# Attention and a two-level mixture of experts on one core: query blocks transposed by VectorE, two PSUM copies on ScalarE, and a reordered end

## The chip, the core and the metric

The kernel runs on one core of a Trainium2 chip. A core has five engines with an instruction stream each: TensorE (PE, matrix products; its weight loads are listed as PEld), VectorE (DVE), ScalarE (ACT), GpSimd (POOL) and SyncE (SP, which here only issues DMAs). They wait for each other by semaphores. SBUF and PSUM are on-chip memories of 128 partitions; matmul results go to PSUM banks, which another engine has to copy out. The metric is the device time of one execution in microseconds (us). The time before is 558.53 us, the median of 3 runs (556.01 to 560.62).

## The reference, cut to what matters

First multi-query attention: 8 batches, 16 query heads, 384 tokens, head size 64, one key head and one value head that all query heads share. Then each of the 3072 tokens (1024 features, the 16 heads side by side) goes to one of 16 experts, chosen in two steps (4 groups, then 4 experts in the group).

```python
scores = scale * np.matmul(q, k.transpose(0, 1, 3, 2))
scores = scores - np.max(scores, axis=-1, keepdims=True)
attn = np.exp(scores)
attn = attn / (np.sum(attn, axis=-1, keepdims=True) + 1e-09)
attn_out = np.matmul(attn, v)
x = attn_out.transpose(0, 2, 1, 3).reshape(B * S, H * D)

g_logits = x @ w_group;  g_idx = argmax;  g_w = softmax(g_logits)[g_idx]
e_logits = x @ w_expert[g_idx];  e_idx = argmax;  e_w = softmax(e_logits)[e_idx]
out = g_w * e_w * (np.maximum(x @ w1[g, e], 0.0) @ w2[g, e])
```

All inputs are float32. With the inputs of this case nearly all tokens of a batch choose the same expert: one expert serves each of the first seven batches, and two serve the last.

## The kernel before, in words

**Tiles and slots.** The 384 tokens of a batch are three tiles of 128, so there are 24 tiles `t`. A tile has eight units (two heads each). The main loop runs over 96 slots `i`; a slot takes two units, so a tile is four slots, p = 0 to 3, and a batch is twelve.

**One slot.** TensorE forms the scores of the two units (L161). VectorE takes the row maxima (L169), ScalarE the exponentials with their sums (L172), VectorE the reciprocals (L183), GpSimd normalises (L187). Two slots later VectorE transposes the normalised rows in 32x32 blocks into a ring buffer (L193); that ring feeds the product with the values. Scores live in two PSUM buffers of two banks, one for each unit of a slot, which TensorE may write again when the exponentials have read them.

**What TensorE does besides.** In slots p = 0 and 1 it advances the expert of the batch before by two or three groups (`advance`; a group is 8 matmuls into one PSUM bank: L419 for the first weights, L433 for the second) and transposes queries (`q_group`, L147). In slots p = 2 and 3 it forms the product of the previous tile with the values (`pv`, L209, 96 matmuls in each of the two slots). All of these but the scores, and later the logits, take their banks in turn from four PSUM banks (`xbank`).

**Queries.** `load_q` brings a tile's queries with tokens on partitions: one DMA of 128 partitions by 16 heads by 64 numbers, into one of three buffers. `q_group` takes eight heads, transposes them pair by pair on TensorE against an identity into PSUM (four transposes), and ScalarE copies the result to SBUF (L151). The half needed later in tile `t` is made in slot 4t, the first half of tile t+1 in slot 4t+1. Tile `j` of a batch holds tokens p*3 + j for p = 0 to 127.

**Keys and values.** `prep_batch` transposes the keys of the next batch on TensorE in a batch's ninth slot; `prep_out` scales them by VectorE on the way out of PSUM (L135). `load_v` brings four copies of the values.

**After a tile's values.** `pv_out` copies four banks with ScalarE (L222), GpSimd casts to bf16 for the experts (L223). `logits` multiplies by the gate weights (L230), `logits_out` copies the result out of PSUM by VectorE (L239), `logits2` sums four partial rows on TensorE (L247), `logits2_out` copies that (L251). The gate functions (L256 to L388) run on VectorE at set slots, and the expert of a batch is picked after its first tile.

**Weights.** `load_w` asks GpSimd's DMA queue for an expert's two matrices (L394), two DMAs of 1 MB each, into two buffers per matrix. For batch b this is done behind slots 12b + 10 (the last batch: the second matrix one slot later). The last batch has a second expert: `load_second(0)` and `load_second(1)`.

**What sets the order.** The order on each engine is written out by hand: `at(slot, where, fn)` files a call under a slot and a letter, `run(slot, where)` makes the calls, and the loop at L603 fixes where the letters stand in a slot: scores, s, b, m0, m1 or values, v, m2, the ring transposes, w, `norm`, g. After the loop (L632 to L662) stands a hand-written end: remaining groups of the expert of batch 6, the last values, the last tile's logits and gate, the experts of batch 7, the second one's results added and stored in six pieces. A loop for further experts follows (L708); it has nothing to do with these inputs.

Of the kernel before, what the change touches and what calls it, by code (L numbers as in the profile page):

```python
# [9 lines left out]
FP32 = mybir.dt.float32  # L10
BF16 = mybir.dt.bfloat16
I32 = mybir.dt.int32
P = 128
AX = mybir.AxisListType
ALU = mybir.AluOpType
# [4 lines left out]
def kernel(  # L20
# [11 lines left out]
    nc = tc.nc  # L32
# [15 lines left out]


    xb_dram = nc.dram_tensor("xb_scratch", [B, P, KO * S], BF16).ap()  # L50
    out_v = out.rearrange("(b p j) d -> b p j d", p=P, j=ST)
    w1f = moe_w1.rearrange("g e (ko ki) f -> (g e) ki ko f", ki=P)
    w2f = moe_w2.rearrange("g e (fo fi) d -> (g e) fi fo d", fi=P)

# [29 lines left out]
    ring = singles.tile([P, 3, 4, 2, S], FP32)  # L84
    NB = S // 32

    def xbank():
        x = ps_x.tile([P, 512], FP32, tag="x", name="x")
        return x
# [5 lines left out]

    def load_q(t, first=False):
        b, j = t // ST, t % ST
        q_sb = qpool.tile([P, H, D], FP32, tag="q", bufs=3)
        qv = q[b].rearrange("h (p j) d -> p j h d", j=ST)
        if first:  # L100
            nc.sync.dma_start(out=q_sb[:, 0:H // 4, :], in_=qv[:, j, 0:H // 4, :])
            nc.scalar.dma_start(out=q_sb[:, H // 4:H // 2, :], in_=qv[:, j, H // 4:H // 2, :])
            nc.sync.dma_start(out=q_sb[:, H // 2:H, :], in_=qv[:, j, H // 2:H, :])
        else:
            nc.sync.dma_start(out=q_sb[:], in_=qv[:, j, :, :])
        st["q", t] = q_sb

    def load_k(b, first=False):
# [23 lines left out]
    def prep_out(b):  # L132
        pt = st.pop(("kt_ps", b))
        kt = qpool.tile([P, S], FP32, tag="kt")
        nc.vector.tensor_scalar(out=kt[:], in0=pt[:, 0:S], scalar1=scale, scalar2=None, op0=ALU.mult)  # L135
        st["kt", b] = kt

    def q_group(t, half, parts=1):
        q_sb = st["q", t]
        half ^= swapped(t)  # L140
        qt = pool.tile([P, 512], FP32, tag="qt", bufs=3)
        n = 4 // parts
        for part in range(parts):
            pt = xbank()
            for c in range(part * n, (part + 1) * n):
                h = 2 * (half * 4 + c)
                nc.tensor.transpose(  # L147
                    out=pt[:, ts(c, P)], in_=q_sb[:, h:h + 2, :].rearrange("p t d -> p (t d)"), identity=ident[:]
                )
            r = slice(part * n * P, (part + 1) * n * P)  # L150
            nc.scalar.copy(out=qt[:, r], in_=pt[:, r])  # L151
        st["qt", t, half] = qt

    def scores(u):
# [81 lines left out]

    def logits_out(b, j):
        lt = pool.tile([P, P], FP32, tag="lt")
        nc.vector.tensor_copy(out=lt[:], in_=st.pop(("lt_ps", b, j))[:, 0:P])  # L239
        if j == 0:  # L240
            st["lg", b] = pool.tile([P, ST, NL], FP32, tag="lg", name="lg")
        st["lt", b, j] = lt
# [228 lines left out]
    def main_expert(b, on_act):  # L471
        w1, w2 = st.pop(("w", b))

        def store(j, y):
            if b < B - 1:
                nc.sync.dma_start(out=out_v[b, :, j, :], in_=y[:])
            else:
                st["y", j] = y

        yield from expert(st["xb", b], w1, w2, scaled(lambda: st["gsel", b][0], store), any_bank, on_act)  # L480

    def second_expert(on_act):

        b = B - 1

        def result(j, nh, yp, by_act):
            y = st["y", j]
            nc.vector.scalar_tensor_tensor(
                out=y[:, ts(nh, 512)], in0=yp, scalar=st["gsel", b][1][:, j:j + 1], in1=y[:, ts(nh, 512)],
                op0=ALU.mult, op1=ALU.add,  # L490
            )
            nc.sync.dma_start(out=out_v[b, :, j, ts(nh, 512)], in_=y[:, ts(nh, 512)])

        yield from expert(st["xb", b], *st.pop("w_second"), result, any_bank, on_act)

# [20 lines left out]
    def at(slot, where, fn, *args):  # L516
        later.setdefault((slot, where), []).append((fn, args))
# [8 lines left out]
    for b in range(B):  # L526
        s0 = SB * b
        for j in range(ST):
            x = s0 + 4 * j + 8
            at(x, "m2", logits, b, j)  # L530
            at(x, "w", logits_out, b, j)
            at(x + 1, "m0", logits2, b, j)
            at(x + 1, "v", logits2_out, b, j)
        for x, j0, j1 in ((s0 + 9, 0, 1), (s0 + 17, 1, ST)):
            at(x, "v", lambda b=b, j0=j0, j1=j1: st.__setitem__(("gm", b), gate_masks(b, j0, j1)))
            at(x, "v", lambda b=b: [next(st["gm", b]) for _ in range(3)])
        if b == 0:
            at(s0 + 10, "s", gate_choose, b)
            at(s0 + 10, "b", gate_score, b)
        else:  # L540
            at(s0 + 9, "m2", gate_choose, b)
            at(s0 + 9, "w", gate_score, b)
        at(s0 + 10, "w", gate_pick, b)
        at(s0 + 10, "g", load_main, b, 0)
        at(s0 + (11 if b == B - 1 else 10), "g", load_main, b, 1)
        at(s0 + 16, "g", keep_xb, b)
        at(s0 + 20, "m0", gate_count, b)
        at(s0 + 20, "v", gate_counted, b)
        x = s0 + (20 if b == B - 2 else 23)
        at(x, "w", lambda b=b: st.__setitem__(("gv", b), gate_values(b)))  # L550
        at(x, "w", lambda b=b: [next(st["gv", b]) for _ in range(3)])
        if b == B - 1:
            at(s0 + 13, "w", gate_pick_second, b)
            at(s0 + 13, "g", load_second, 0)
        if b + 1 < B:
            at(s0 + 4, "g", load_k, b + 1)
            at(s0 + 4, "g", load_v, b + 1)
            at(s0 + 8, "m0", prep_batch, b + 1)
            at(s0 + 8, "v", prep_out, b + 1)
    for t in range(NT):  # L560
        at(4 * t, "m1", q_group, t, 1)
        if t + 1 < NT:
            at(4 * t + 1, "m1", q_group, t + 1, 0)
        if 1 <= t < NT - 2:
            at(4 * t, "g", load_q, t + 2)

    load_k(0, first=True)
# [31 lines left out]
    busy(1)  # L599
    q_group(0, 0, 2)  # L600
    load_v(0)
    load_q(2)
    for i in range(NSL):  # L603
        t, p = i // 4, i % 4
        if i >= SB + 5 and (i - 5) % SB == 0:
            pending.append(main_expert((i - 5) // SB - 1, lambda k: True))
        us = (2 * i, 2 * i + 1)
        for u in us:
            scores(u)
        run(i, "s")  # L610
        soft(us, lambda: run(i, "b"))
        if p < 2:
            run(i, "m0")
            advance(1)
            run(i, "m1")
            advance(2 if p == 1 and t % ST > 0 else 1)
        elif t > 0:
            pv(t - 1, (p - 2) * NB // 2, (p - 1) * NB // 2)
        run(i, "v")
        run(i, "m2")  # L620
        if i >= 2:
            transp(2 * i - 4)
            transp(2 * i - 3)
        run(i, "w")
        norm(us)
        if p == 3 and t > 0:
            pv_out(t - 1)
        run(i, "g")
# [10 lines left out]
    run(i, "w")  # L639
    transp(2 * i - 2)  # L640
    transp(2 * i - 1)
    advance(1)
    run(i + 1, "m0")
    run(i + 1, "v")
    run(i + 1, "w")
    run(i + 1, "g")
    pv(NT - 1, 0, NB)
    pv_out(NT - 1)
    advance(2)
    run(i + 4, "m2")  # L650
    run(i + 4, "w")
    run(i + 4, "g")
    advance(1)
    run(i + 5, "m0")
    run(i + 5, "v")
    pending.append(main_expert(b, lambda k: k < FO or k % 2 == 0))
    advance(1)
    load_second(1)
    pending.append(second_expert(None))
    advance(2)  # L660
    run(i + 8, "m0")
    run(i + 8, "v")  # L662

# [44 lines left out]
    with tc.For_i(0, n_rem, 1) as it:  # L708
        free.clear()
        e = nc.gpsimd.value_load(lse[0:1, ds(it, 1)], min_val=0, max_val=GE - 1)  # L710
        w1, w2 = load_w(e, 0), load_w(e, 1)
        bi = nc.sync.value_load(lsb[0:1, ds(it, 1)], min_val=0, max_val=B - 1)
        xr = pool.tile([P, KO, S], BF16, tag="xb", name="xr", bufs=2)
        nc.sync.dma_start(
            out=xr[:].rearrange("p c t -> p (c t)"), in_=xb_dram[ds(bi, 1)].rearrange("o p c -> (o p) c")
        )
        pid = nc.vector.value_load(lsi[0:1, ds(it, 1)], min_val=0, max_val=NP - 1)
        gcol = pool.tile([P, ST], FP32, tag="gcol")
        nc.vector.tensor_copy(out=gcol[:], in_=grem_all[:, ds(pid, 1), :].rearrange("p o j -> p (o j)"))
        bp = nc.gpsimd.value_load(lsb[0:1, ds(it, 1)], min_val=0, max_val=B - 1)  # L720

        def add(j, y):
            nc.gpsimd.dma_start(
                out=out_v[ds(bp, 1), :, j, :].rearrange("o p d -> (o p) d"), in_=y[:], accum_op=ALU.add
            )

        for _ in expert(xr, w1, w2, scaled(lambda: gcol, add), bank_end):
            pass
# [30 lines left out]
```

## Time and profile before

| what | value |
|---|---|
| median of 3 runs | 558.53 us |
| the profiled execution, its own time | 560.02 us |
| its span, first to last instruction | 558.58 us |
| TensorE (PE) busy | 530.6 us, 95% |
| VectorE (DVE) busy | 418.4 us, 75% |
| ScalarE (ACT) busy | 339.2 us, 61% |
| GpSimd (POOL) busy | 270.6 us, 48% |
| mean granted TensorE clock | 0.991 |
| moved by DMA | 75.15 MB |
| median from issue to landing: a tile's queries, 512 KB | 6.4 us |
| median from issue to landing: 1 MB of weights | 18.7 us |

The page lists for each group of instructions its source line, engine, operation, output and input tiles, their shapes, the count, then busy time and mean duration, then the engine's idle time just before them and what ended it. The chain is followed back from the last instruction: at each step to what released it, or else to the instruction before it on its engine; "issue" is time in which an engine waited for nothing that the profile shows. Matmuls are pipelined: on the chain a piece counts from its start to the start of the next. The windows view lists busy time of each engine in a stretch, then the granted clock, the share of the DMA engines and what they moved.

### The profile page before, as it was taken

The page shows a single profiled execution, that of the slowest core. Times are in us where ns is not written, and L with a number is a line of the kernel's source. Part 1 is how long each engine was busy: PE and PEld are TensorE (multiplying, and loading weights), DVE is VectorE, ACT ScalarE, POOL GpSimd, SP SyncE. Part 2 cuts the span into 40 slices and gives each one's busy share as a digit, 9 for nine tenths or more (in the row PEclk, how much of TensorE's full clock was granted, in tenths as well). Part 3 has the DMA queues.
Part 4 walks back from the last instruction along what each step waited for, and adds up shares of the span by engine and source line. Part 5 has one row for each costly group of instructions (what it writes and reads, how often), then busy time and mean ns, then how long its engine had stood idle before and what let it go on. Part 6 is the DMA issues. An engine that isn't in the chain of part 4 may idle for free.

```text
span 558.6 us, 17530 instructions
## 1 busy us (share of the span) xinstructions
PE 530.6 (95%) x7074; PEld 310.1 (56%) x7074; DVE 418.4 (75%) x847; ACT 339.2 (61%) x1043; POOL 270.6 (48%) x456
## 2 busy tenths in 40 slices
PE   7598899999999999999999999999999999979994
PEld 3255456655665556655665556655665555555452
DVE  4989988877888778877888678876888778823322
ACT  4776666666666666766666676676666676613210
POOL 2655954564457444565447535555447535622000
PEclk9999999999999999999999999999999999989999
DMA  7710993099805993099706992199706960299923
GB/s 118 161 30 13 177 229 75 2 195 233 202 2 97 210 250 77 4 200 247 181 1 111 213 262 48 11 211 247 164 2 111 213 189 2 29 212 263 222 51 115
DMA packets 98098, 75.15 MB, mean 135 GB/s; under 512 B 75104, under 2 KB 75104, under 8 KB 98016
## 3 DMA queue, kind: packets, MB, share of 16 engines
q0 software_dynamic: 19008, 37.75, 38.1%
q1 hardware_dynamic: 78080, 36.04, 24.7%
q8 instruction: 57, 0.93, 0.7%
q10 hardware_dynamic: 928, 0.23, 0.2%
q14 instruction: 25, 0.20, 0.1%
HBM read 92.88 MB, written 18.87 MB: 200 GB/s over the span
## 4 chain that ended last, share of the span: by engine, by line
PE 88%; DVE 6%; ACT 3%; issue 2%; ACTq 0%; DVEq 0%
PE x L209 24%; PE s L161 22%; PE x L419 13%; PE x L433 11%; PE sb L433 6%; PE sb L419 4%; PE x L147 3%; DVE nmx L169 3%; ACT pr L172 3%; PE x L230 2%; DVE ring L193 2%; PE x L247 1%; PE x L94 1%; PE x L129 0%; PE x L338 0%
## 5 line engine op out<-in xcount | busy, mean ns | idle before, releaser
L187 POOL TENSOR_SCALAR pr<-pr,rinv 128x384 f32<-128x384 f32 x384 | 218.2, 591 | 222.6 <-DVE rinv L183 222.6
L172 ACT ACTIVATE pr<-s,nmx 128x384 f32<-128x384 f32 x384 | 217.9, 580 | 139.6 <-DVE nmx L169 133.1
L169 DVE TENSOR_REDUCE nmx<-s 128x2 f32<-128x768 f32 x192 | 174.4, 948 | 58.0 <-PE s L161 57.8
L193 DVE STREAM_TRANSPOSE ring<-pr 128x768 f32<-128x768 f32 x192 | 175.4, 952 | 0.0
L161 PE MATMUL s<-kt,qt 64*128 64x384 f32 x768 | 152.8, 511 | 13.0 <-ACT pr L172 12.8
L209 PE MATMUL x<-ring,v_sb 32*64 32x256 f32 x4608 | 142.5, 382 | 5.8 <-issue 4.8
L209 PEld LDWEIGHTS x<-ring,v_sb 32*64 32x64 f32 x4608 | 103.5, 132 | 47.8 <-issue 28.9
L161 PEld LDWEIGHTS s<-kt,qt 64*128 64x128 f32 x768 | 65.1, 186 | 71.5 <-ACT pr L172 37.3
L419 PE MATMUL x<-xb,w 128*128 128x384 bf16 x448 | 79.5, 326 | 0.0
L172 ACT ACTIVATION_READ_ACCUMULATOR pr<-s,nmx 128x1 f32 x384 | 77.9, 203 | 0.0
L419 PEld LDWEIGHTS <-w 128*128 128x128 bf16 x576 | 56.6, 100 | 32.0
L433 PEld LDWEIGHTS <-h_t 128*128 128x128 bf16 x432 | 41.3, 100 | 50.4 <-issue 9.1
L433 PE MATMUL x<-w,h_t 128*128 128x512 bf16 x288 | 68.2, 379 | 0.0
L222 ACT COPY xt<-x 128x256 f32<-128x256 f32 x96 | 29.1, 391 | 13.5 <-PE x L209 13.1
L425 ACT ACTIVATE h_t<-x 128x384 bf16<-128x384 f32 x56 | 28.2, 506 | 9.4 <-PE x L419 8.8
L433 PE MATMUL sb<-w,h_t 128*128 128x512 bf16 x144 | 33.2, 388 | 0.0
L394 POOL DMA_DIRECT2D w<-in_moe_w_dram x36 | 27.5, 777 | 10.5 <-PE x L247 5.6
L151 ACT COPY qt<-x 128x512 f32<-128x512 f32 (+1 forms) x49 | 29.0, 594 | 2.7 <-PE x L147 2.7
L239 DVE COPY lt<-x 128x128 f32<-128x128 f32 x24 | 6.7, 278 | 31.7 <-PE x L230 31.6
L147 PE MATMUL x<-ident,q_sb 128*128 128x128 f32 x192 | 29.5, 277 | 0.0
L147 PEld LDWEIGHTS x<-ident,q_sb 128*128 128x128 f32 x192 | 23.7, 143 | 8.9 <-issue 1.6
L223 POOL CAST xb<-xt 128x1024 bf16<-128x1024 f32 x24 | 24.9, 1040 | 7.5 <-ACT xt L222 7.5
(83 smaller groups left out, 217.5 us busy)
## 6 DMA issues: line engine op xcount, KB each, us to landing
w<-in_moe_w_dram POOLq DMA_DIRECT2D x36, 1024.0 KB, 18.7
q_sb<-in_q_dram SPq DMA_DIRECT2D x23, 512.0 KB, 6.4
out_dram<-y SPq DMA_DIRECT2D x21, 512.0 KB, 8.3
xb_scratch<-xb SPq DMA_DIRECT2D x8, 768.0 KB, 5.5
v_sb<-in_v_dram SPq DMA_DIRECT2D x32, 96.0 KB, 4.2
out_dram<-y SPq DMA_DIRECT2D x6, 256.0 KB, 2.0
kk<-in_k_dram SPq DMA_DIRECT2D x15, 96.0 KB, 5.4
q_sb<-in_q_dram SPq DMA_DIRECT2D x1, 256.0 KB, 4.1
```

The lines of the kernel that those rows point to most:

```text
L147: nc.tensor.transpose(out=pt[:, ts(c, P)], in_=q_sb[:, h:h + 2, :].rearrange("p t d -> p (t d)"), identity=ident[:])
L151: nc.scalar.copy(out=qt[:, r], in_=pt[:, r])
L161: nc.tensor.matmul(out=s[:, h, 0:S], lhsT=qt[r, ts(cc, P)], rhs=kt[r, :], start=True, stop=True)
L169: nc.vector.tensor_reduce(out=nmx[:], in_=s[:, :, 0:S], axis=AX.X, op=ALU.max, negate=True)
L172: nc.scalar.activation(out=pr[:, h, :], in_=s[:, h, 0:S], func=ACTF.Exp, bias=nmx[:, h:h + 1], scale=1.0, accum_out=ssum[:, k, h:h + 1],)
L187: nc.gpsimd.tensor_scalar(out=pr, in0=pr, scalar1=rinv[:, k, h:h + 1], scalar2=1.0, op0=ALU.mult, op1=ALU.mult)
L193: nc.vector.transpose(out=ring[:, (u // 4) % 3, u % 4].rearrange("p h s -> p (h s)"), in_=st.pop(("pr", u))[:].rearrange("p h s -> p (h s)"),)
L209: nc.tensor.matmul(out=o[i][h * D:(h + 1) * D, 0:2 * P].rearrange("d (g c q) -> d g c q", g=2, c=4), lhsT=v_sb[r, n, :], rhs=ring[r, a:z + ...
L222: nc.scalar.copy(out=xt[:, :, ts(i, 32)], in_=o[:, 0:2 * P].rearrange("p (c q) -> p c q", c=KO))
L419: nc.tensor.matmul(out=hp[:, 0:S], lhsT=w1[:, ko, ts(fc, P)], rhs=xb[:, ko, :], start=(ko == 0), stop=(ko == KO - 1))
L425: nc.scalar.activation(out=h_t[:, fc, :], in_=hp[:, 0:S], func=ACTF.Relu)
L433: nc.tensor.matmul(out=yp, lhsT=h_t[:, fo, ts(j, P)], rhs=w2[:, fo, ts(nh, 512)], start=(fo == 0), stop=(fo == FO - 1),)
```

## The change

- The queries of tiles 6 to 23 are loaded in another arrangement: partition 32i + r holds, for the eight heads of one parity (i // 2), the four tokens 4r to 4r+3, from the first or second half of the head's 64 numbers on (i % 2). A DMA piece is 224 neighbouring numbers, 896 bytes; four DMAs make a tile. VectorE then transposes 32x32 blocks (`q_blocks`, one instruction per eight heads, 512 elements per partition, reading 32 of every 64), straight from SBUF to SBUF. These tiles have no transposes on TensorE and no copy on ScalarE. The call stands behind the reciprocals (new letter e).
- Tiles 0 to 5 keep TensorE's transposes. Their loads are four DMAs of 32 partitions each; the first tile's are eight, on two queues.
- A tile now holds 128 neighbouring tokens, with partition 32n + r for token 4r + n. The output view `out_v` follows. The first tile of a batch, from which its expert is picked, thus holds other tokens; with these inputs the pick is the same.
- Query buffers: two of twice the size instead of three. The load of tile t + 2 stands behind slot 4t for all tiles, tile 2 among them.
- The first copy of the logits and, except for batch 0, the scaling of the keys are done by ScalarE, the latter at letter w instead of v.
- In the end part: two groups of batch 6's expert more stand ahead of the last values; the request for the second expert's first matrix moves from ahead of the last values to behind them; the main expert of batch 7 is made available one call earlier.

```diff
-    out_v = out.rearrange("(b p j) d -> b p j d", p=P, j=ST)
+    QN = P // 32
+    out_v = out.rearrange("(b j r n) d -> b j n r d", j=ST, n=QN, r=32)
...
+    TQ = 6
...
-        q_sb = qpool.tile([P, H, D], FP32, tag="q", bufs=3)
-        qv = q[b].rearrange("h (p j) d -> p j h d", j=ST)
-        if first:
-            nc.sync.dma_start(out=q_sb[:, 0:H // 4, :], in_=qv[:, j, 0:H // 4, :])
-            nc.scalar.dma_start(out=q_sb[:, H // 4:H // 2, :], in_=qv[:, j, H // 4:H // 2, :])
-            nc.sync.dma_start(out=q_sb[:, H // 2:H, :], in_=qv[:, j, H // 2:H, :])
+        q_sb = qpool.tile([P, 2 * H * D], FP32, tag="q", bufs=2)
+        if t < TQ:
+            q_sb = q_sb[:, 0:H * D].rearrange("p (h d) -> p h d", h=H)
+            qv = q[b].rearrange("h (j r n) d -> j n r h d", n=QN, r=32)
+            for h0 in range(0, H, H // 2 if first else H):
+                for n in range(QN):
+                    (nc.scalar if first and n % 2 else nc.sync).dma_start(
+                        out=q_sb[32 * n:32 * (n + 1), h0:h0 + (H // 2 if first else H), :],
+                        in_=qv[j, n, :, h0:h0 + (H // 2 if first else H), :],
+                    )
         else:
-            nc.sync.dma_start(out=q_sb[:], in_=qv[:, j, :, :])
+            q_sb = q_sb[:].rearrange("p (c x) -> p c x", c=H // 2)
+            qv = q[b].rearrange("(c h) (j r n) d -> h j r c (n d)", h=2, n=QN, r=32)
+            for i in range(4):
+                nc.sync.dma_start(
+                    out=q_sb[32 * i:32 * (i + 1), :, 0:QN * D - 32],
+                    in_=qv[i // 2, j, :, :, 32 * (i % 2):32 * (i % 2) + QN * D - 32],
+                )
...
-        nc.vector.tensor_scalar(out=kt[:], in0=pt[:, 0:S], scalar1=scale, scalar2=None, op0=ALU.mult)
+        if b == 0:
+            nc.vector.tensor_scalar(out=kt[:], in0=pt[:, 0:S], scalar1=scale, scalar2=None, op0=ALU.mult)
+        else:
+            nc.scalar.mul(out=kt[:], in_=pt[:, 0:S], mul=scale)
...
+    def q_blocks(t, half):
+        half ^= swapped(t)
+        qt = pool.tile([P, 512], FP32, tag="qt", bufs=3)
+        q_sb = st["q", t][:, 4 * half:4 * (half + 1), :].rearrange("p c (n d) -> p (c n) d", n=QN)
+        nc.vector.transpose(out=qt[:].rearrange("p (x d) -> p x d", d=32), in_=q_sb[:, :, 0:32])
+        st["qt", t, half] = qt
...
-        nc.vector.tensor_copy(out=lt[:], in_=st.pop(("lt_ps", b, j))[:, 0:P])
+        nc.scalar.copy(out=lt[:], in_=st.pop(("lt_ps", b, j))[:, 0:P])
...
-            at(s0 + 13, "g", load_second, 0)
...
-            at(s0 + 8, "v", prep_out, b + 1)
+            at(s0 + 8, "w", prep_out, b + 1)
...
-        at(4 * t, "m1", q_group, t, 1)
-        if t + 1 < NT:
-            at(4 * t + 1, "m1", q_group, t + 1, 0)
-        if 1 <= t < NT - 2:
+        for x, u, half in ((4 * t, t, 1), (4 * t + 1, t + 1, 0)):
+            if u < TQ:
+                at(x, "m1", q_group, u, half)
+            elif u < NT:
+                at(x, "e", q_blocks, u, half)
+        if t < NT - 2:
             at(4 * t, "g", load_q, t + 2)
...
         norm(us)
+        run(i, "e")
...
-    advance(1)
+    advance(2)
     run(i + 1, "m0")
     run(i + 1, "v")
     run(i + 1, "w")
-    run(i + 1, "g")
+    advance(1)
     pv(NT - 1, 0, NB)
     pv_out(NT - 1)
+    load_second(0)
     advance(2)
     run(i + 4, "m2")
     run(i + 4, "w")
     run(i + 4, "g")
+    pending.append(main_expert(b, lambda k: k < FO or k % 2 == 0))
     advance(1)
     run(i + 5, "m0")
     run(i + 5, "v")
-    pending.append(main_expert(b, lambda k: k < FO or k % 2 == 0))
     advance(1)
     load_second(1)
     pending.append(second_expert(None))
-    advance(2)
+    advance(1)
```

## The prediction

> **What bounds the kernel now.** I read the page first: busy shares, then the chain that ended last.
>
> ```profile
> PE 530.6 (95%) x7074; PEld 310.1 (56%) x7074; DVE 418.4 (75%) x847; ACT 339.2 (61%) x1043; POOL 270.6 (48%) x456
> ...
> PE 88%; DVE 6%; ACT 3%; issue 2%; ACTq 0%; DVEq 0%
> ```
>
> TensorE is busy for 95% and is 88% of the chain. A share is an average, so I read the chain piece by piece. This is a slot p = 0 (a slot is four heads of 128 queries) and, below the dots, the first half of a tile's values in the slot after next; columns start, us, what:
>
> ```profile
> 236.28 1.49 PE s L161 x8
> 237.77 1.83 PE x L433 x8
> 239.61 0.44 PE x L147 x4
> 240.04 1.73 PE x L433 x8
> 241.77 0.57 PE x L230 x16
> 242.34 1.49 PE s L161 x8
> ...
> 249.55 2.78 PE x L209 x96
> ```
>
> Pieces join without a gap: from about 77 to 465 us TensorE works back to back, and a transpose group (L147) costs the path 0.44 us, not the 0.6 us from its first start to its last end, because it overlaps its neighbours. Three stretches differ. Up to 77 us no expert runs and DVE and ACT take turns with PE. At 465 to 472 us DVE leads. And in the tail:
>
> ```profile
> 489.54 0.29 DVE lt L239
> 489.83 1.74 DVE ring L193 x2
> 491.57 0.10 DVE lg L251
> 491.67 0.05 issue
> 491.72 4.11 PE x L209 x135
> 495.83 2.92 issue
> 498.75 3.69 PE x L209 x57
> 502.44 4.66 PE sb L433 x16
> ```
>
> The last 192 value matmuls should take 2 x 2.78 = 5.56 us and the two W2 groups behind them 3.56 (as the same two took at 485.34). They took from 491.72 to 507.10, 15.38 us: **6.3 us lost**, of which 2.92 is a hole. The rest is the clock, by windows:
>
> ```profile
> 496.00:499.00 3.00, 0.25 (x8) 0.25 (x15) 0.00 (x0) 0.00 (x0) 0.00 (x0) 0.80 1.11 244
> 499.00:501.00 2.00, 2.00 (x48) 1.73 (x44) 0.00 (x0) 0.00 (x0) 0.00 (x0) 0.50 1.12 211
> ```
>
> Columns after the length are PE, PEld, DVE, ACT and POOL busy, granted clock, DMA share, GB/s. The DMA engines are full and the clock falls to 0.50 after the hole.
>
> **The change, part by part.** The sum is made against the profiled execution: 560.02 us, a span of 558.58 and 1.44 around it. It lies 1.5 above the median of the runs, 558.53.
>
> *Transposes off TensorE.* 18 of 24 tiles, two groups each: 36 groups x 0.44 = **-15.8 us**, all in slots that PE fills. On ACT 36 copies of 604 ns go, 21.7 us, worth nothing by themselves since ACT waits 133 us for maxima anyway.
>
> *Block transposes on DVE.* 36 new instructions of 128x512 with a strided source. No row shows this shape. Nearest:
>
> ```profile
> L193 DVE STREAM_TRANSPOSE ring<-pr 128x768 f32<-128x768 f32 x192 | 175.4, 952 | 0.0
> L151 ACT COPY qt<-x 128x512 f32<-128x512 f32 (+1 forms) x49 | 29.0, 594 | 2.7 <-PE x L147 2.7
> L239 DVE COPY lt<-x 128x128 f32<-128x128 f32 x24 | 6.7, 278 | 31.7 <-PE x L230 31.6
> ```
>
> In sequence the L193 pair takes 1.75, so 0.875 each; two thirds of that is 0.58. If the stride halved the rate, 1.2. I take 0.6, as it reads and writes as many elements per cell as the dense one. Does DVE hold it? I added its pitches per slot: maxima 1.75, ring 1.75, reciprocal 0.08, and extras: masks 1.35, counts 1.1, pick 0.9, gate values 1.4. A batch (12 slots) is 62.7 us of PE and becomes 60.0; DVE needs 49 and gets 6 x 0.6 = 3.6 more. So there are 7 us of slack, but unevenly spread: value slots last 4.27, the two expert slots 5.6 and 5.7 after the cut. Lag arises in the batch's third value slot (4.49 against 4.27) and its fourth (1.75+1.75+1.4+0.08 = 5.0 against 4.27): now 0.9 us at 238.09, where the maximum starts 1.9 after the scores and not 1.0. The score buffer tolerates 0.7 (ACT ends at 256.54, the next second scores need it at 257.36). The next expert slot then needs 0.95 + 3.6 + 0.6 = 5.2 of 5.6, so the lag is gone after one slot. Behind the block transposes on DVE stand the next slot's maxima, for which ACT waits. Some tenths per batch may leak through: I charge **+1 us** (0 to 7, the upper end with 1.2 us apiece).
>
> *First logits copy to ACT.* DVE loses 24 x 0.28 us of work and 31.6 us of waiting for PE (14.9 of it once, in the tail). On ACT the same wait stands behind the expert's evacuations and ahead of the next exponentials, which start 1.2 to 2.7 us later still. By the nearest ACT row, 391 ns for 256 elements, a copy is 0.2 to 0.39. L247 needs it 1.49 us after the logits end: covered, by 0.5 us in the tightest slot. Where DVE led it pays: 0.5 us at 472 (L247 waited for lt behind the gate values), 0.4 at 491 (the ring behind lt). With *key scaling on ACT* (0.47 us of DVE at 39.44, and the lt wait at 41.57) the early slots gain 0.7. Together **-1.6 us**; bounds 0 and -3.
>
> *Loads.* A late q tile becomes four DMAs of 256 pieces of 896 bytes, where it was one of 2048 pieces of 256: 0.92 MB for 0.52, half the pieces. Two buffers instead of three make SP wait for the block transpose of tile t before it asks for t+2, at the end of the same slot where it asked before, so nothing new queues behind that wait but one output store. SP issues cost 0.4 to 0.8 us, three more per tile. The worst load is issued among the weights (243.59) and lands after 21 us; it is needed about 25 us after its issue. Full DMA ends when the weights do, so more bytes can add 1 or 2 us, fewer pieces take some away: 0. The start has eight q issues on two queues where it had three; the second on each begins near 2.6 us and by the 3.2 to 3.8 us of landing arrives near 6.1, where PE needs it at 5.90: **+0.2** (0 to 0.7). The early loads of tile 2 and of batch 1, which now stand in their slots, still land (4 to 5 us) before their use. Stores keep one DMA per tile and 4 KB rows: 0.
>
> *The tail.* Five groups instead of three stand ahead of the last values, so one instead of three behind them; group time only moves. Behind the values ACT copies (1.4) and POOL casts (1.04): 2.6 us, against 1.73 + 0.57 of PE work: **+0.3**. The second expert's first weights are asked for some 10 us later, land about 15 us after that, and are used 21 us after the main expert starts: covered by some 5 us. The main expert's own weights (asked at 484.57, landing after 12) are there.
>
> What becomes of the 6.3 us? The edit takes the POOL request of 494.18 away from the hole at 495.83. But I doubt that request as the cause. Instruction blocks come by DMA too (queue 8: 57 packets, 0.93 MB, so 16 KB each). Counting PE's instructions in the trace, every hole inside value matmuls, at 68.45, 192.27, 317.32, 380.48 and this one, lies at the same place modulo 256 (193 or 194). In the loop those holes are 0.4 to 0.6 us, since scores stretch the block; here a whole block is value matmuls, used up in 3.7 us, while under full DMA a block arrives some 4.5 us after its predecessor is entered, plus 0.9 for the packet and 1.6 until work resumes. The earlier weights keep the DMA full until about 507 whether or not the third request is there. Removing 36 x 8 = 288 instructions plus some waits, and moving 32 ahead, leaves the boundary 10 to 50 instructions into the values: again a whole block in them. What does help is that DVE no longer holds PE's queue at 491.6, so the block can be asked for about 1.4 us earlier. I take a hole of 1.5 to 2.5 us without the clock's fall: **-4**; bounds -6.3 (no hole) and 0.
>
> The Trainium skill, page "Runtime: NRT & Kernel Launch", section "Instruction fetch mechanics", says that an engine's instructions are refilled in 16 KiB blocks of 256 and calls the cost of crossing "mostly hidden". The trace agrees on the block and not on the hiding: 2.92 us. By that sentence the moved request could give nothing here and the sum would be 4 us worse or, with no hole at all, 2 us better.
>
> *Sum:* -15.8 + 1 - 1.6 + 0.2 + 0.3 - 4 = -19.9, so 540.1 against 560.02; against the median, 538.6. I say **539 us**.
>
> **Rivals.**
> 1. *The hole and the half clock stay* (0.25). A hole near 2.9 us, then 6.8 us of half clock, as now. For it: the boundary, the full DMA. Against: the earlier request. The tail gives 0, so 543. The Trainium skill, "TensorE: Matmul & The Clock Gate", section "What's actually happening", puts the fall after an idle window of about 3.4 us that runs freely; the trace's fall at 497.8, 2 us into the hole, and its 6.8 us of 0.50 agree, so chance decides whether a shorter hole trips it.
> 2. *The hole goes altogether* (0.2): the third request was the cause. -6.3, so 536.5.
> 3. *DVE becomes the near bound* (0.13): block transposes at 1.2 us or lag that leaks in each of six batches, 1 to 2 us each: 545 to 550.
> 4. *Slower* (0.06): the strided block transpose runs at a quarter of the dense rate. From 10.6 / 6 = 1.8 us apiece DVE is the longest engine of a batch; at 2.8 us it needs 49 + 17 = 66 of 62.7 and the kernel takes some 6 x 3.3 - 4 = 16 us more: 575. Against: L193 is the same operation at full rate, and its blocks are 32 wide too.
> 5. *The change does less than it says* (0.04): late q tiles in the weights' shadow stall DVE once a batch by several us and eat the gain: 553 to 560.
>
> **How the numbers follow.** My forecast has 0.32, between rivals 1 and 2, which differ from it in the tail alone. 1% (5.6 us) is about what a measurement can tell from no change. Faster by more than that are the forecast and rivals 1, 2, 3: 0.90. Rival 5 is half no change, half a small gain; slower keeps 0.06, no change 0.04. The range reaches from 534 (no hole, a little luck with the loop's holes) to 547 (half of rival 3), leaving out about 0.2.
>
> **What would show it.** L147 with 48 in place of 192, and chain pieces of L433 or L419 joining across its place in the loop: a batch of about 60 us. A DVE row of 36 block transposes near 0.6 to 0.75 us mean. Waits of PE for ACT's exponentials no longer than now (50 us in all). lt on ACT near 0.3. In the tail, value matmuls with or without an "issue" piece and a clock row of 0.50. Wrong if PE waits grow in the value slots, or if a DMA of q appears among DVE's releasers.

## The result: 582.3 us, slower

| | before | changed |
|---|---|---|
| median | 558.18 us (555.87 to 560.62) | 582.28 us (581.88 to 584.33) |
| profiled execution, its span | 560.02, 558.58 us | 584.33, 582.89 us |
| TensorE busy | 530.6 us | 525.7 us |
| mean granted TensorE clock | 0.991 | 0.966 |

The ratio is 1.0443, with a 95% interval of 1.0414 to 1.0471. The prediction said 539 us, within 534 to 547.

### The profile page after: what moved, and what is told of

It is laid out like the page before. It is cut to its first block, busy times and chain, and to the rows that moved or that the text cites. A ratio compares the mean times of both kernels' runs of the same rounds, so it can differ in the third digit from the quotient of the medians.

```text
span 582.9 us, 17319 instructions
## 1 busy us (share of the span) xinstructions
PE 525.7 (90%) x6930; PEld 295.2 (51%) x6930; DVE 429.6 (74%) x852; ACT 329.9 (57%) x1038; POOL 269.7 (46%) x456
## 4 chain that ended last, share of the span: by engine, by line
PE 52%; DMA 27%; DVE 8%; SPq 3%; POOL 3%; ACT 2%; issue 2%; POOLq 0%; ACTq 0%; DVEq 0%
PE x L234 14%; PE s L186 14%; DMA kk<-in_k_dram 13%; DMA q_sb<-in_q_dram 9%; PE x L444 8%; PE x L458 7%; DMA w<-in_moe_w_dram 6%; PE sb L458 4%; DVE nmx L194 3%; DVE ring L218 3%; ACT pr L197 2%; POOL pr L212 2%; PE sb L444 2%; SPq L125 2%; PE x L255 1%
## 5 line engine op out<-in xcount | busy, mean ns | idle before, releaser
L186 PE MATMUL s<-kt,qt 64*128 64x384 f32 x768 | 155.0, 516 | 11.5 <-ACT pr L197 11.2
L234 PE MATMUL x<-ring,v_sb 32*64 32x256 f32 x4608 | 140.1, 379 | 2.6 <-issue 1.7
L444 PE MATMUL x<-xb,w 128*128 128x384 bf16 x448 | 83.2, 345 | 0.0
L444 PEld LDWEIGHTS <-w 128*128 128x128 bf16 x576 | 58.8, 104 | 38.5 <-issue 6.7
L458 PE MATMUL x<-w,h_t 128*128 128x512 bf16 x288 | 65.2, 379 | 0.0
L450 ACT ACTIVATE h_t<-x 128x384 bf16<-128x384 f32 x56 | 26.0, 499 | 32.2 <-PE x L444 32.1
L248 POOL CAST xb<-xt 128x1024 bf16<-128x1024 f32 x24 | 24.8, 1035 | 11.1 <-ACT xt L247 11.1
L176 DVE STREAM_TRANSPOSE qt<-q_sb 128x512 f32<-128x512 f32 x36 | 24.9, 692 | 3.6 <-DMA q_sb<-in_q_dram 3.3
L476 ACT ACTIVATE y<-x,gsel 128x512 f32<-128x512 f32 x36 | 24.3, 696 | 3.8 <-PE x L458 3.8
L444 PE MATMUL sb<-xb,w 128*128 128x384 bf16 x128 | 21.6, 326 | 0.0
L476 ACT ACTIVATE y<-sb,gsel 128x512 f32<-128x512 f32 x9 | 6.2, 688 | 24.0 <-PE sb L458 24.0
```

The lines of the kernel that those rows point to most:

```text
L186: nc.tensor.matmul(out=s[:, h, 0:S], lhsT=qt[r, ts(cc, P)], rhs=kt[r, :], start=True, stop=True)
L234: nc.tensor.matmul(out=o[i][h * D:(h + 1) * D, 0:2 * P].rearrange("d (g c q) -> d g c q", g=2, c=4), lhsT=v_sb[r, n, :], rhs=ring[r, a:z + ...
L444: nc.tensor.matmul(out=hp[:, 0:S], lhsT=w1[:, ko, ts(fc, P)], rhs=xb[:, ko, :], start=(ko == 0), stop=(ko == KO - 1))
L450: nc.scalar.activation(out=h_t[:, fc, :], in_=hp[:, 0:S], func=ACTF.Relu)
L458: nc.tensor.matmul(out=yp, lhsT=h_t[:, fo, ts(j, P)], rhs=w2[:, fo, ts(nh, 512)], start=(fo == 0), stop=(fo == FO - 1),)
L476: nc.scalar.activation(out=y[:, ts(nh, 512)], in_=yp, func=ACTF.Copy, scale=g)
```

## The profile after

The page of the changed kernel, its busy shares, one DMA queue (packets, MB, share of 16 engines) and the chain that ended last:

```profile
PE 525.7 (90%) x6930; PEld 295.2 (51%) x6930; DVE 429.6 (74%) x852; ACT 329.9 (57%) x1038; POOL 269.7 (46%) x456
...
q1 hardware_dynamic: 59948, 42.99, 29.1%
...
PE 52%; DMA 27%; DVE 8%; SPq 3%; POOL 3%; ACT 2%; issue 2%; POOLq 0%; ACTq 0%; DVEq 0%
PE x L234 14%; PE s L186 14%; DMA kk<-in_k_dram 13%; DMA q_sb<-in_q_dram 9%; PE x L444 8%; PE x L458 7%; DMA w<-in_moe_w_dram 6%; PE sb L458 4%; DVE nmx L194 3%; DVE ring L218 3%; ACT pr L197 2%; POOL pr L212 2%; PE sb L444 2%; SPq L125 2%; PE x L255 1%
```

Before, no transfer was on the chain at all and TensorE was 88% of it. Now transfers are 27%: of keys (kk), queries and weights. The chain piece by piece (start, us, what) says which ones:

```profile
59.73 23.38 DMA q_sb<-in_q_dram
83.25 1.08 PE x L164 x4
...
141.46 2.27 POOL pr L212 x4
143.73 0.86 SPq L435
145.32 16.10 DMA kk<-in_k_dram
161.56 0.87 PE x L143 x3
162.43 3.79 PE x L444 x16
...
445.42 23.52 DMA q_sb<-in_q_dram
469.07 0.71 DVE qt L176
...
501.58 33.91 DMA w<-in_moe_w_dram
535.50 0.04 issue
535.54 11.94 PE sb L458 x44
```

They are one query load early (tile 5), the keys of five later batches at 14 to 16 us each (before, their median was 5.4 us from issue to landing), one late query load, for which VectorE's block transposes wait, and one megabyte of the last weights after 34 us. That megabyte is half of the second matrix of batch 7's main expert. The waits view (us in total, times, longest) has the two largest, keys and weights:

```profile
PEld x L143 <- ACT pr L197: 14.6, 5, 3.6
...
PE x L143 <- DMA kk<-in_k_dram: 14.1, 5, 3.5
...
PE sb L458 <- DMA w<-in_moe_w_dram: 8.9, 1, 8.9
```

The first two rows are the weight loads and the matmuls of the same five key transposes: TensorE stands still for about 2.8 us in each of five batches. At the end of four of these waits the granted clock falls to 0.50 for 3.4 us (from 161.3, 226.2, 291.0 and 355.9 us on). By estimate each fall costs up to 1.7 us more, half of 3.4. In the wait for the weights it falls too, to 0.50 for 10.2 us from 529.9 us on.

What held the keys up? They are asked on SP's queue behind two output stores and the copy of a batch's tokens (768 KB). Windows of the changed kernel (length, busy PE, PEld, DVE, ACT, POOL, granted clock, DMA share, GB/s), first while the stores run almost alone, then over the end of a key wait:

```profile
150.00:152.00 2.00, 2.00 (x88) 1.75 (x80) 2.00 (x3) 1.55 (x5) 0.89 (x2) 1.00 0.25 104
152.00:154.00 2.00, 2.00 (x38) 0.81 (x26) 1.67 (x4) 0.81 (x4) 0.88 (x2) 1.00 0.25 104
...
160.00:166.00 6.00, 4.44 (x19) 2.53 (x19) 2.93 (x6) 1.53 (x5) 2.59 (x5) 0.72 0.96 191
```

A DMA share of 0.25 is **four engines of 16**. Counted packet by packet, those of 4096 bytes, which are the stores', keep 4.1 engines busy from 148 to 156 us. The keys behind them on the queue wait, and from 150 to 154 us the other 12 engines are nearly idle. The two stores take 10.7 us in all (147.2 to 157.9); in the kernel before, the same two took 3.8 (137.6 to 141.4). The view `(b j r n) d -> b j n r d` is why: in DRAM order the store of a tile now begins with a dimension of 4 (n), then 32 rows, where it began with 128 rows. The Trainium skill, page "DMA: Bandwidth & Descriptors", section "Why a DMA increments its semaphore by 16 and not by 1", says that a DMA is spread over the largest number of engines up to 16 that divides the slowest dimension of both its sides; 4 and 128 give 4. The trace agrees: 4.1.

Where the 24.3 us of span went, by the starts of scores in the slots and the last matmul:

| stretch | before | changed | difference |
|---|---|---|---|
| start to slot 20 | 90.4 | 96.4 | +6.0 |
| slots 20 to 92 | 374.5 | 380.4 | +5.8 |
| slot 92 to the last matmul | 86.2 | 91.1 | +4.9 |
| from there to the end (last stores) | 7.4 | 15.0 | +7.6 |

## The experiments

The theory S from here on: the stores' four engines are the loss, by keys that queue behind them, weights that share those engines, and the last stores themselves. Rivals: the block transposes cost more than they save; the loads of queries are late; the reordered end is at fault. Times are medians beside the kernel before on the same chip, 557.0 to 558.1 us; ratios are against it, with 95% intervals.

**Stores as four DMAs of 32 rows.**

```diff
-                nc.sync.dma_start(out=out_v[b, j], in_=y[:])
+                for n in range(QN):
+                    nc.sync.dma_start(out=out_v[b, j, n], in_=y[32 * n:32 * (n + 1), :])
...
```

The six half-tile stores of the last batch are split in the same way.

> The changed kernel, but each output store is four DMAs of 32 rows (one for each n) in place of one whose slowest dimension has size 4. Theory S (the changed output view puts each store on 4 of the 16 DMA engines; keys and weights queued behind and beside it come late): the share of engines that 4096-byte packets keep busy rises from a steady 4.1 towards 16 when nothing else runs, the waits of TensorE for keys (14 us before its matmuls and as much before its weight loads) and for the expert weights (8.9 us) vanish, and the time falls from 582 to 540-548. Rival Q (the query loads, 0.92 MB in place of 0.52, hold up the queue): keys still land after 14-16 us, time 575-583. Rival D (VectorE became the bound): no change, 580-583.

Measured: 545.66 us (544.75 to 546.34), ratio 0.9773 [0.9753, 0.9793]. The same bytes, rows and places as in the changed kernel cost **36.6 us less**. DMA issues of this kernel (count, KB each, median us to landing), and its chain where the keys' wait was:

```profile
out_dram<-y SPq DMA_DIRECT2D x84, 128.0 KB, 6.5
...
kk<-in_k_dram SPq DMA_DIRECT2D x15, 96.0 KB, 3.7
```

```profile
158.34 0.35 PE x L363 x2
158.69 0.35 PE x L143 x3
159.04 2.60 PE x L444 x16
```

Keys land in 3.7 us, and their transposes join their neighbours with no transfer between. The query loads and the block transposes are as in the changed kernel, so rivals Q and D fall. By the stretches above: slots 20 to 92 take 356.8 us (-17.7 against before), the stretch after -5.6, the end +1.9; the start keeps +6.1.

**The other way round: the kernel before with these stores alone.**

```diff
+    out_n = out.rearrange("(b j r n) d -> b j n r d", j=ST, n=4, r=32)
...
-                nc.sync.dma_start(out=out_v[b, :, j, :], in_=y[:])
+                nc.sync.dma_start(out=out_n[b, j], in_=y[:])
...
```

> The kernel before with the changed output view in its stores alone; everything else, queries included, is as before. Its output rows are therefore in another order within a tile. Theory S: the stores alone cost most of what the change lost: keys land after 12 us or more, the last weights late, 570-585. Rivals Q and D: the stores are the same bytes in the same 4096-byte pieces, 556-561.

Measured: 579.02 us, ratio 1.0384 [1.035, 1.0419]. On its chain (as above) stand keys, two late query loads and weights that were not on the chain of the kernel before:

```profile
141.17 14.09 DMA kk<-in_k_dram
204.56 14.25 DMA kk<-in_k_dram
268.16 14.58 DMA kk<-in_k_dram
...
372.87 23.16 DMA q_sb<-in_q_dram
...
436.35 23.07 DMA q_sb<-in_q_dram
...
501.17 41.37 DMA w<-in_moe_w_dram
```

So the view alone makes the kernel slower by 21 us, without any of the other edits. The end part loses 12.6 us here (+5.0 and +7.5), as in the changed kernel; slots 20 to 92 lose only 6.9 where the changed kernel loses 23.5 against the split stores. Most of that difference is in the keys: here TensorE's transposes wait 1.7 us for them in all, 0.8 at most, against 14.1, and no half clock follows. The keys land after 14.1 to 14.6 us here and after 14.0 to 16.1 there; why the changed kernel waits so much longer for them was not separated further.

**No block transposes, stores split.** `TQ = 24` in place of 6.

> As the kernel with split stores, but all 24 tiles keep TensorE's transposes (256-byte query pieces, copies on ScalarE): the block transposes are taken away. If the transposes off TensorE are worth 36 x 0.44 us and VectorE holds the new work, this is 13 to 17 us slower than the kernel with split stores. Rival D: it is no slower, or faster. Two query buffers alone may make loads late in the weights' shadow once a batch (256-byte pieces took 21 us there), which would add some us more.

Measured: 561.08 us, ratio 1.0059 [1.0034, 1.0083]. Against the split stores alone, 15.4 us more: the block transposes bring what they were to bring. The query loads do not blur this: TensorE waits for them 3.8 us here and 4.5 with the split stores alone, most of it (3.6 and 3.5) in one wait for tile 5. Without the block transposes the rest of the change is worth nothing or slightly less.

**Tile 5 in large pieces too, stores split.** `TQ = 5`.

> As the kernel with split stores, but tile 5 too is loaded in 896-byte pieces and transposed by VectorE. In the changed kernel tile 5's 256-byte pieces, asked for among the first weights at 59.7 us, landed after 23.4 us, TensorE waited 3.9 us and its clock was halved for 3.4 us. If the number of pieces sets the time in the weights' shadow (half as many here) the wait goes: 2 to 5 us faster than with split stores alone. If the bytes set it, the same or slower.

Measured: 542.07 us, ratio 0.9689 [0.9658, 0.972]; 3.6 us less than with `TQ = 6`. This is tile 5's load, asked at 59.73 in the changed kernel and at 39.16 before, when there was a third buffer. As 2048 pieces of 256 bytes it needs 23 us among the weights; in the profiled runs TensorE's waits for queries go from 4.5 to 0.7 us. The 3.6 us are not all that the late load costs: a stop of 2.2 us with 3.4 us of half clock behind it, in the scores of slot 19, is new here. The last experiment is about such stops.

**The request for the second expert's weights back ahead of the last values.** Stores split.

```diff
+    load_second(0)
     advance(1)
     pv(NT - 1, 0, NB)
     pv_out(NT - 1)
-    load_second(0)
```

> The kernel with split stores, but the second expert's first weights are asked for ahead of the last values again. Theory B (the hole in the last values of the kernel before came from a 16 KB instruction block that was late under full DMA, wherever the third request stood): a hole of 0 to 1 us as with split stores alone, clock 1.0 through the last values, time within 2 us of 545.7. Rival P (the third request made the hole): a hole near 2.9 us at half clock, 4 to 6 us slower.

Measured: 545.39 us, ratio 0.9776 [0.9742, 0.981]: no difference from 545.66 that can be measured. The stop in the last values is 0.89 us (0.16 with split stores alone), and the clock stays full. With this end part, where the request stands decides nothing.

**The whole end part as before.** Stores split.

> The kernel with split stores, with the whole end part as before (three groups of batch 6's expert ahead of the last values, not five, and the third request ahead of them). Theory B with the earlier asking (two groups more ahead let the block be asked for earlier): the hole grows again to 1.5 to 3 us, with or without the half clock: 2 to 6 us slower than with split stores. Rival P: the same 4 to 6, so this run tells only together with the one that moves the request alone. If the end part does nothing: within 1 us.

Measured: 547.96 us, ratio 0.9817 [0.9783, 0.9852]: 2.3 us more. The gap in the last values, from one weight load's start to the next, is 3.31 us here, with 3.4 us of half clock behind it; with the new end part it was 0.74 and the clock stayed full. The intervals of the two ratios overlap, so 2.3 is a rough size; in the profiled runs the stretch from slot 92 to the last matmul is 3.4 us longer.

**Logits copy and key scaling back on VectorE.** Stores split.

```diff
-        nc.scalar.copy(out=lt[:], in_=st.pop(("lt_ps", b, j))[:, 0:P])
+        nc.vector.tensor_copy(out=lt[:], in_=st.pop(("lt_ps", b, j))[:, 0:P])
```

> The kernel with split stores, with the first logits copy and the key scaling on VectorE as before. The prediction put their move at 1.6 us in all (0 to 3), and the wait of VectorE for the logits (31.6 us before) now stands ahead of the block transposes: 1.5 to 6 us slower than with split stores.

Measured: 545.03 us, ratio 0.9777 [0.9749, 0.9805]. Nothing was lost by taking the move back; the expectation, 1.5 to 6 us, was wrong, and so was the prediction's term.

**Rows put back in token order on the chip, so that a store is one DMA of 128 rows.** With `TQ = 5`, the ordering done by GpSimd's cast and, in the same way, for the logits by ScalarE's copy.

```diff
-    out_v = out.rearrange("(b j r n) d -> b j n r d", j=ST, n=QN, r=32)
+    out_v = out.rearrange("(b j p) d -> b j p d", j=ST, p=P)
...
-        nc.gpsimd.tensor_copy(out=st["xb", b][:, :, ts(j, P)], in_=xt[:])
+        nc.gpsimd.tensor_copy(
+            out=st["xb", b][:, :, ts(j, P)].rearrange("p c (r n) -> p c n r", n=QN),
+            in_=xt[:].rearrange("p c (n r) -> p c n r", n=QN),
+        )
...
```

> Block transposes from tile 5 on; the rows are put back in order where GpSimd casts (its output written with stride 4) and where ScalarE copies the logits, so that each output store is one DMA of 128 whole rows, with no new DMA. Theory S: stores on 16 engines as before the change, the last store again some 2 us quicker than with four DMAs: 2 to 4 us below the 542.1 of four DMAs with tile 5, 537-541, if the strided cast stays near 1.04 us. If GpSimd's strided writing takes twice that, POOL (50% busy) still has room: within 1 us of the same.

Measured: 542.10 us, ratio 0.973 [0.9701, 0.9759]. The end is short again (7.1 us), but the cast (busy us, mean ns, idle before) takes 2.4 times its 1035 ns:

```profile
L248 POOL CAST xb<-xt 128x1024 bf16<-128x1024 f32 x24 | 59.8, 2490 | 10.6 <-ACT xt L247 10.6
```

**The same order made by ScalarE's copy instead.**

```diff
-            nc.scalar.copy(out=xt[:, :, ts(i, 32)], in_=o[:, 0:2 * P].rearrange("p (c q) -> p c q", c=KO))
+            nc.scalar.copy(out=xt[:].rearrange("p c (r n) -> p c n r", n=QN)[:, :, i, :], in_=o[:, 0:2 * P].rearrange("p (c q) -> p c q", c=KO))
```

> The changed kernel with tile 5 in 896-byte pieces too, and with the 128 token rows put back in natural order by ScalarE's copy of the value banks (it writes every fourth number) instead of GpSimd's cast, so that each store is one DMA whose slowest dimension is 128. What each theory expects: if only GpSimd pays for a stride (2.49 us against 1.04 in the run with the rows put in order by the cast), the ScalarE copies stay near 0.39 us, the cast goes back to about 1.04, keys land within 8 us, and the time is 537 to 541, 1 to 5 us under that run's 542.1. If ScalarE pays for the stride as GpSimd did (2.4 times, so about 0.95 us a copy, 2.2 us more for a tile ahead of its logits), the time is 541 to 546.

Measured: 539.16 us (537.0 to 540.26), ratio 0.9645 [0.9609, 0.9682].

```profile
L247 ACT COPY xt<-x 128x256 f32<-128x256 f32 x96 | 48.8, 672 | 11.1 <-PE x L234 10.8
L248 POOL CAST xb<-xt 128x1024 bf16<-128x1024 f32 x24 | 24.8, 1035 | 15.0 <-ACT xt L247 15.0
```

ScalarE does pay for the stride, 672 ns against 390, less than GpSimd; the time is that of the first theory, the duration lies between the two. With one DMA for a store over 128 rows the end is 6.7 us, against 9.6 with four DMAs in the run with `TQ = 5`.

**TensorE's instructions shifted by 55 pairs.** The kernel above, with 60 short dummy matmuls in place of five of the seven long ones that it runs while the first keys come:

```diff
-    busy(7)
+    busy(2, 60)
```

> The kernel with the rows ordered by ScalarE, and at its start 60 short dummy matmuls more and 5 long ones fewer: 55 pairs of weight load and matmul more ahead of everything. They stand where TensorE waits for the first keys. If the holes in the value matmuls are instruction blocks that arrive late, the boundary inside the last values moves from pair 156 to about pair 101 of 192, the block before it then holds some 27 pairs of the slow second-weight groups and lasts over 6 us, and the 2 us hole in the last values is gone (no gap over 0.4 us) while all holes left elsewhere still stand at 193 or 194 modulo 256; the time is 1 to 3 us less. If the hole is set by the traffic or by data at that time, a gap of 1 to 3 us stays in the last values, not at pair 101, and the time is the same within 1 us.

Measured: **535.67 us** (534.51 to 536.05), ratio 0.9593 [0.9563, 0.9623]; 3.5 us less for 55 instruction pairs more. TensorE's timeline over the last values (start, us, what), first of the kernel above, then of the shifted one:

```profile
479.68 4.55 PE L234 MATMUL x<-ring,v_sb 32*64 32x256 f32 x155
485.83 1.51 PE L234 MATMUL x<-ring,v_sb 32*64 32x256 f32 x37 [1.60 <-issue]
```

```profile
475.97 5.43 PE L236 MATMUL x<-ring,v_sb 32*64 32x256 f32 x192
```

The 192 matmuls run through, in 5.43 us; the prediction had put them at 5.56 without a hole. A second hole went with it: at 86.5 us the kernel above waits 1.62 us for nothing shown in the scores of slot 19, and has 3.4 us of half clock behind it; that stop, too, is at place 193 modulo 256. By spans, 538.72 to 533.86, 3.8 us of the 4.9 are gained before slot 20 and 1.3 between slot 92 and the last matmul. The holes that are left inside value matmuls (from the weight loads that start at 70.29, 186.3, 247.71 and 425.17 us to the next ones; 0.5 to 1.0 us), counted over all instructions of TensorE, are again at 193. Most crossings of that place pass without a stop, so it takes a late block as well. The packets of the instruction queue show the lateness: one of 16 KB runs from 483.45 to 484.40 us in the kernel above, and the values go on at 485.83; in the kernel before one runs from 496.26 to 497.15, and they go on at 498.75. In all the holes named here work resumes 1.2 to 1.7 us after such a packet has ended. Late instruction blocks are the cause of these holes, which the prediction had argued and these runs show.

## Why the prediction was wrong, by its own steps

The step that failed is one sentence under *Loads*: "**Stores keep one DMA per tile and 4 KB rows: 0.**" Both halves hold, and the conclusion does not: the rows and the bytes stayed, but the order of dimensions took 12 of 16 engines from each store. The term measures +36.6 us (the changed kernel against the same with split stores), more than all the gains together; in the kernel before the same view costs 21. The prediction read the view as a matter of which rows, not of how the DMA is spread. The forecast's sign was lost here alone: with the stores split, the change is faster by 2.3%.

The other terms, against the split stores where a run has them:

- *Transposes off TensorE, -15.8, and the leak of DVE's lag, +1:* right. Together -14.8 was said, -15.4 measured (`TQ = 24` against 6).
- *Block transposes at 0.6 us, bounds 0.58 and 1.2:* near. The row has 692 ns, and DVE carried it; rivals 3 and 4 fall, and the sign that rival 4 shared with the result came from another cause. The prediction's warning, a query DMA among DVE's releasers, did come, for rival 5's reason, a late query load, but it is small: 3.3 us of waiting in the changed kernel, none with the stores split:

```profile
L176 DVE STREAM_TRANSPOSE qt<-q_sb 128x512 f32<-128x512 f32 x36 | 24.9, 692 | 3.6 <-DMA q_sb<-in_q_dram 3.3 <-issue 0.3
...
L264 ACT COPY lt<-x 128x128 f32<-128x128 f32 x24 | 6.6, 277 | 0.7
```

- *Logits copy and key scaling, -1.6:* wrong, about 0 by the run that moves both back. The ScalarE copy costs what was said (277 ns); the gain was put together from single waits of VectorE, and a wait taken away there did not move the end.
- *The early loads "still land before their use":* wrong for tile 5, +3.6 us. The prediction checked the late loads of 896-byte pieces against their 25 us and did not check the one small-piece load that the lost buffer had moved 20 us later, into the weights. In the last kernel, where the stop that took its place is gone as well, slot 20 starts 0.6 us earlier than in the kernel before, not 6 later.
- *The start, +0.2:* the first scores begin 0.5 us later (7.3 against 6.8), inside the bounds.
- *The main expert's weights of batch 7, "are there":* wrong in the changed kernel for the second matrix, by the store's engines (8.9 us of waiting); nearly right with the stores split, where the same megabyte lands after 25 us and TensorE waits 0.7.
- *The tail, -4 + 0.3:* the sign was right; the size is 2.3 us by the times, 3.4 by the traces, against 3.7 forecast. In the changed kernel the boundaries lie where they were forecast, about 38 and 294 instructions into the values (the stop stands behind 147 pairs). The hole there is shorter than the 1.5 to 2.5 us forecast, with the clock at 1.00, but its gain was buried under the late weights:

```profile
505.89 4.53 PE L234 MATMUL x<-ring,v_sb 32*64 32x256 f32 x147
510.85 1.54 PE L234 MATMUL x<-ring,v_sb 32*64 32x256 f32 x45 [0.43 <-issue]
```

- *Rival 1, hole and half clock stay:* falls with the new end part; with the old one both are there. The prediction lets the clock's fall at 497.8 agree with an idle stretch of about 3.4 us, but it came 2.0 us into the hole, and a stop of 1.62 us was followed by one too.
- *Rival 2, the third request as the cause of the hole:* falls; putting it back changes no time, and moving the boundary alone removes the hole.

The kernel with ordered rows, in which stores are one DMA over 128 rows and tile 5's load comes in large pieces, has a span 19.9 us below that of the kernel before, and 539.16 us. That it meets the sum is partly chance: it has no late tile 5, no gain from the copies, a hole that costs 2.2 us in the last values and another in slot 19.

## What to carry to other kernels

When an edit changes the view that a DMA reads or writes, look at the slowest dimension of both sides before bytes and rows: 128 became 4 here, and one store held up everything behind it on its queue. Price a lost buffer at each load that it moves, the odd ones first. Holes without a named releaser on an engine with thousands of short instructions can be counted modulo the block (256 here), held against the packets of the instruction queue, and moved by shifting the stream, for the price of a few dummy instructions in time that waits anyway.

## What the runs showed of the hardware that was not expected

- Two 512 KB stores over four engines run for 10.7 us, at a DMA share of 0.25 where little else moves (3.8 us before), and 96 KB of keys behind them on the same queue land after 14 to 16 us instead of 3.7 to 7.5. Transfers on another queue suffer too: a megabyte of weights asked at 500.8 us landed at 535.5, while the median of its kind was 23.0 us against 18.7 before.
- Four waits of TensorE for keys, of 2.6 to 3.4 us, were each followed by 3.4 us of half clock, which by estimate makes them half as dear again; the fifth, of 2.1 us, was not. A stop of 1.62 us elsewhere was. So the length alone does not decide.
- A 16 KB block of TensorE's instructions can come late while the DMA engines are busy: work resumed 1.2 to 1.7 us after its packet, and the stops measured 0.4 to 3.3 us.
- Writing every fourth element costs GpSimd's cast 2490 ns instead of 1035 for 128x1024, ScalarE's copy 672 instead of 390 for 128x256. A 32x32-block transpose that reads 32 of every 64 elements costs VectorE 692 ns for 128x512, next to 952 for 128x768 without gaps: 9% more per element.
